# A pointwise convolution whose start is rearranged: weights, first rows and their queues

## The chip, the core and the metric

The kernel runs on one core of a Trainium2 chip. Its engines work side by side and are ordered by semaphores: TensorE (PE) multiplies matrices, VectorE (DVE) and ScalarE (ACT) move and convert data, GpSimd (POOL) does small side work, and SyncE (SP) issues most of the transfers. ScalarE can issue transfers too, on a queue of its own. The metric is the device time of one execution in microseconds (us). It is measured several times and the median is taken.

## The reference: what is computed

A depthwise convolution with a 1x1 window is a scaling of each channel, so the whole reference is one matrix product with scaled rows:

```python
# x: (1, 384, 384, 384) bf16, dw: (1, 1, 384), pw: (384, 384)
out = x * dw[0, 0]                              # k = 1: no neighbours, a scale for each channel
out = jnp.einsum('bhwc,cd->bhwd', out, pw)      # 147456 rows of 384, times a 384x384 matrix
```

There are N = 147,456 rows. The kernel folds `dw` into `pw` once and then multiplies every row of `x` by the folded 384x384 matrix.

## The kernel before

The rows are worked on in supertiles of 512 rows; there are NS = 288 of them. For each one the DVE transposes `x` (32x32 blocks of 32-bit words, so two bf16 channels stay together), TensorE runs 48 matmuls that accumulate in four PSUM banks, and ScalarE copies the result to SBUF as bf16. Both the transposed tile `T` and the PSUM tile `PS` exist twice. Groups of supertiles are loaded as chunks of `x` and stored from tiles `O`:

```python
def _groups(n_super):
    head, tail = [[1, 1, 2, 2, 4]], [[6, 4], [4, 1, 1, 1, 1]]
    mid = n_super - sum(map(sum, head + tail))
    return head + [[LMAX]] * (mid // LMAX) + tail      # LMAX = 10; a number is supertiles in a chunk
```

Before the first supertile the weights have to be made. `pw` comes in thirds of 128 rows, `dw` as one row. TensorE turns the `dw` row into a column, one matmul for each third; the DVE multiplies a selection matrix by it (`sel_w`); TensorE multiplies `sel_w` by `pw`, which scales, picks and replicates the rows. That gives six pieces (third k, parity r), which are copied from PSUM to `w_r`.

```python
# SyncE's queue, and one transfer on ScalarE's
nc.scalar.dma_start(dw_row[:], ...).then_inc(s_dw, 16)
nc.sync.dma_start(pw_n[:, 0], pw[0:P, :]).then_inc(s_pw, 16)
nc.sync.dma_start(pw_n[:, 1:3], pw[P:C, :]...).then_inc(s_pw2, 16)
load_x(0)
...
# TensorE, in order of its program
idle_work(4)                       # 16 matmuls on constants
nc.tensor.wait_ge(s_dw, 16)
... three matmuls of dw_row -> PS[1][:, 0, D:D+3], then_inc(s_df)
idle_work(2)
nc.tensor.wait_ge(s_pw, 16)
times = {(2, 0): 2, (2, 1): 2}     # the last third's matmuls are run twice
for k in range(3):
    if k == 1: nc.tensor.wait_ge(s_pw2, 16)
    nc.tensor.wait_ge(s_sw, k + 1)             # sel_w of this third
    for r in range(2):
        if k == 2: nc.tensor.wait_ge(*w_done[r])   # PSUM is free again
        for v in [0, 1] * times.get((k, r), 1):
            nc.tensor.matmul(PS[(k + 1) % 2][:, 2 * r + v, :D],
                             lhsT=sel_w[64 * v : 64 * v + 64, k, r, :, :]..., rhs=pw_n[64 * v : 64 * v + 64, k, :], ...)
        mm.then_inc(s_w)
with nc.tensor.Fori(0, NS // 2 - 1, 1) as it: ...     # supertiles, 48 matmuls each
```

In a supertile the matmuls go through twelve steps (channel block b, parity), four matmuls in each. The waits stand in it like this:

```python
w_first = {(0, 0): [(0, 1), (1, 3)], (4, 0): [(1, 4)], (4, 1): [(1, 5)]}   # step: (engine, pieces done)
for b, par in steps:        # (0,0), (0,1), (1,0), ... (3,1), (4,0), (5,0), (4,1), (5,1)
    for q in range(4):
        if q == 0 and par == 0 and b in (0, 3): nc.tensor.wait_ge(s_t[s][b // 3], rv)   # T's halves
        if q == 0 and s == 0:
            for e, v in w_first.get((b, par), []): nc.tensor.wait_ge(s_wr[e], v)
        nc.tensor.matmul(PS[s][:, q, :D], lhsT=Ts[s][...], rhs=w_r[...], ...)
```

The pieces are copied by ScalarE, except for the second, which the DVE takes (`w_eng = [1, 0, 1, 1, 1, 1]`). The DVE's program at the start is: `sel`, the copy of `dw` out of PSUM, three `sel_w`, its piece, and then the transposes, two halves of three channel blocks for each supertile:

```python
nc.vector.tensor_copy(dw_f[:], PS[1][:, 0, D : D + 3])
for k in range(3):
    nc.vector.tensor_scalar_mul(sel_w[:, k], sel..., dw_f[:, k : k + 1]).then_inc(s_sw)
for i in range(6): w_out(i)
transposes(*order[0]); transposes(*order[1])
```

Of the kernel before, what the change touches and what calls it, by code (L numbers as in the profile page):

```python
# [8 lines left out]
F32 = mybir.dt.float32  # L9
# [3 lines left out]
LMAX = 10  # L13
# [3 lines left out]

def _groups(n_super: int):

    head, tail = [[1, 1, 2, 2, 4]], [[6, 4], [4, 1, 1, 1, 1]]  # L20
    mid = n_super - sum(map(sum, head + tail))
    assert mid > 0 and mid % LMAX == 0
    return head + [[LMAX]] * (mid // LMAX) + tail
# [3 lines left out]
def kernel(  # L27
# [12 lines left out]
    nc = tc.nc  # L40
    P = nc.NUM_PARTITIONS
    B, H, W, C = x.shape
    assert dw.shape[0] == 1 and dw.shape[1] == 1, "only k=1 depthwise supported"
    D = pw.shape[1]
# [10 lines left out]
    chunks, first = [], 0  # L55
# [13 lines left out]
    consts = ctx.enter_context(tc.tile_pool(name="consts", bufs=1))  # L69
# [4 lines left out]
    pw_n = raw[:, 0 : 3 * D].rearrange("p (k d) -> p k d", d=D)  # L74
    sel_w = raw[:, 3 * D :].rearrange("p (k r q w) -> p k r q w", r=2, q=4, w=32)
    w_k = raw[:, 0 : 2 * D].rearrange("p (r d) -> p r d", d=D)
    eye = consts.tile([P, P], BF16, name="eye")
    sel = consts.tile([P, 2, 32], F32, name="sel")
    w_r = consts.tile([P, NB, 2, D], BF16, name="w_r")
    dw_row = consts.tile([1, C], BF16, name="dw_row")  # L80
    dw_f = consts.tile([P, 3], F32, name="dw_f")
    warm = consts.tile([P, 2], F32, name="warm")

    ones = nc.const_aps.tensor(1.0, [P, D], BF16)
# [6 lines left out]
    PS = [psum.tile([P, 4, 512], F32, name=f"ps{s}") for s in range(2)]  # L91
# [5 lines left out]
    s_t = [[nc.alloc_semaphore(f"s_t{i}{h}") for h in range(2)] for i in range(2)]  # L97
# [2 lines left out]
    s_d = nc.alloc_semaphore("s_d")  # L100
    s_o = [nc.alloc_semaphore(f"s_o{i}") for i in range(NR)]
    s_dw = nc.alloc_semaphore("s_dw")
    s_pw = nc.alloc_semaphore("s_pw")
    s_pw2 = nc.alloc_semaphore("s_pw2")
    s_df = nc.alloc_semaphore("s_df")
    s_sw = nc.alloc_semaphore("s_sw")
    s_dwf = nc.alloc_semaphore("s_dwf")
    s_sel = nc.alloc_semaphore("s_sel")
    s_w = nc.alloc_semaphore("s_w")
    s_wr = [nc.alloc_semaphore(f"s_wr{e}") for e in range(2)]  # L110

    with tc.tile_critical(sync_engine=mybir.EngineType.Pool, no_gpsimd_drain=True):  # L112
# [59 lines left out]
            eng.dma_start(dst, src).then_inc(s_o[g % NR], 16)  # L172

        w_eng = [1, 0, 1, 1, 1, 1]
        w_all = [(s_wr[e], w_eng.count(e)) for e in range(2)]

        nc.scalar.dma_start(dw_row[:], dw.rearrange("a e c -> a (e c)")).then_inc(s_dw, 16)
        nc.sync.dma_start(pw_n[:, 0], pw[0:P, :]).then_inc(s_pw, 16)  # L178
        nc.sync.dma_start(pw_n[:, 1:3], pw[P:C, :].rearrange("(k p) d -> p k d", p=P)).then_inc(s_pw2, 16)  # L179
        load_x(0)  # L180

        todo = []
# [3 lines left out]
            for k in range(n_parts[t] - (first + 1 == NS)):  # L186
                todo.append((first + L * (k + 1) // n_parts[t] + 1, store, (t, k)))
        for _, f, a in sorted(todo, key=lambda a: a[0]):
            if f is load_x and chunks[a[0]][4] == LMAX and chunks[a[0]][0] == 1:
                nc.sync.wait_ge(x_of(1)[1], 16)  # L190
            if f is store and a == (0, 0):

                for _ in range(28):
                    nc.sync.wait_ge(s_pw, 16)
            f(*a)
# [7 lines left out]

        w_done = [(s_wr[e], w_eng[: i + 1].count(e)) for i, e in enumerate(w_eng)]

        w_first = {(0, 0): [(0, 1), (1, 3)], (4, 0): [(1, 4)], (4, 1): [(1, 5)]}

        def w_ps(i):
            return PS[0 if i in (2, 3) else 1][:, 2 * (i % 2) : 2 * (i % 2) + 2, :D]
# [4 lines left out]
        def supertile(s, rv):  # L214
            for b, par in steps:
                for q in range(4):
                    if q == 0 and par == 0 and b in (0, 3):
                        nc.tensor.wait_ge(s_t[s][b // 3], rv)
                    if q == 0 and s == 0:
                        for e, v in w_first.get((b, par), []):  # L220
                            nc.tensor.wait_ge(s_wr[e], v)
                    mm = nc.tensor.matmul(  # L222
                        PS[s][:, q, :D],
                        lhsT=Ts[s][32 * q : 32 * q + 32, b, par::2],
                        rhs=w_r[32 * q : 32 * q + 32, b, par, :],
                        start=(b, par) == steps[0],
                        stop=(b, par) == steps[-1],
                        tile_position=(32 * q, 0),
                    )
                    if (b, par) == steps[0] and q == 0:  # L230
                        mm._wait_ge(s_a[s], rv)
                    if (b, par) in ((2, 1), (5, 1)) and q == 3:
                        mm.then_inc(s_pe)


        def idle_work(n):
            for _ in range(n):
                for i in range(4):
                    nc.tensor.matmul(  # L239
                        PS[0][:, 2 * (i % 2) + i // 2, :D],  # L240
                        lhsT=ones[32 * i : 32 * i + 32, 0:P],
                        rhs=ones[32 * i : 32 * i + 32, :],
                        start=True,
                        stop=True,
                        tile_position=(32 * i, 0),
                    )

        idle_work(4)

        nc.tensor.wait_ge(s_dw, 16)  # L250
        for k in range(3):
            mm = nc.tensor.matmul(
                PS[1][:, 0, D + k : D + k + 1],
                lhsT=dw_row[:, P * k : P * k + P],
                rhs=ones[0:1, 0:1],
                start=True,
                stop=True,
            )
# [2 lines left out]
        nc.tensor.wait_ge(s_pw, 16)  # L261
        times = {(2, 0): 2, (2, 1): 2}
        for k in range(3):
            if k == 1:
                nc.tensor.wait_ge(s_pw2, 16)
            nc.tensor.wait_ge(s_sw, k + 1)
            for r in range(2):
                if k == 2:
                    nc.tensor.wait_ge(*w_done[r])

                for v in [0, 1] * times.get((k, r), 1):
                    mm = nc.tensor.matmul(  # L272
                        PS[(k + 1) % 2][:, 2 * r + v, :D],
                        lhsT=sel_w[64 * v : 64 * v + 64, k, r, :, :].rearrange("p q w -> p (q w)"),
                        rhs=pw_n[64 * v : 64 * v + 64, k, :],
                        start=True,
                        stop=True,
                        tile_position=(64 * v, 0),
                    )
                mm.then_inc(s_w)  # L280
# [22 lines left out]
        for m in range(4):  # L303
# [14 lines left out]
            out=eye[:],  # L318
            in_=ones[:, 0:P],
# [12 lines left out]
        for n in range(4):  # L332
            for g in range(4):
                x_b = Xl[quads[g], n, 256:384].rearrange("p (b c) -> p b c", c=64)
                nc.gpsimd.tensor_copy(Xk[quads[n], g:8:4, :], x_b).then_inc(s_xk)  # L335
                nc.gpsimd.tensor_copy(Xk[quads[n], 8 + g : 24 : 4, :], Xl[quads[g], :, 64 * n : 64 * n + 64]).then_inc(s_xk)  # L336
        for s in range(2):
            nc.scalar.copy(warm[:, s : s + 1], nc.const_aps.tensor(0.0, [P, 1], F32)).then_inc(s_a[s])  # L338

        def transposes(t, j):  # L340
            g, i, off, first, L = chunks[t]
            jj = first + j
            s = jj % 2
            if jj + 1 == NS:
                nc.vector.wait_ge(s_xk, 32)
                Tw = Ts[s][:].bitcast(U32).rearrange("p b (m w) -> p (b m) w", w=32)
                for v in range(2):
                    blocks = slice(12 * v, 12 * v + 12)
                    ins = nc.vector.transpose(out=Tw[:, blocks], in_=Xk[:, blocks].bitcast(U32))  # L349
                    ins._wait_ge(s_pe, 2 * (jj - 2) + v + 1)  # L350
                    ins.then_inc(s_t[s][v])
                return
            X, sem, n = x_of(t)
            Xw = X.bitcast(U32).rearrange("p (k l) c -> p k l c", l=L)
            Tw = Ts[s][:].bitcast(U32).rearrange(
                "p b (k i) -> p b k i" if t < 2 else "p b (i k) -> p b k i", k=4
            )
            for h in range(2):
                if h == 0 and j == 0:
                    nc.vector.wait_ge(sem, n)  # L360
                ins = nc.vector.transpose(  # L361
                    out=Tw[:, 3 * h : 3 * h + 3],
                    in_=Xw[:, :, j, 96 * h : 96 * h + 96].rearrange("p k (b w) -> p b k w", w=32),
                )
                if jj >= 2:
                    ins._wait_ge(s_pe, 2 * (jj - 2) + h + 1)
                ins.then_inc(s_t[s][h])
# [6 lines left out]
        def w_out(i):  # L374
            e, k, r = w_eng[i], i // 2, i % 2
            out, in_ = w_r[:, 2 * k : 2 * k + 2, r, :], w_ps(i)
            o = nc.vector.tensor_copy(out, in_) if e == 0 else nc.scalar.copy(out, in_)  # L377
            o._wait_ge(s_w, i + 1)
            o.then_inc(s_wr[e])
# [3 lines left out]
            out=sel[:],  # L383
            in_=eye[:].rearrange("p (v w r) -> p r w v", v=2, r=2),
            op=mybir.AluOpType.add,
            axis=mybir.AxisListType.X,
        ).then_inc(s_dwf)
        nc.vector.wait_ge(s_df, 1)
        nc.vector.tensor_copy(dw_f[:], PS[1][:, 0, D : D + 3]).then_inc(s_dwf)
        nc.vector.wait_ge(s_dwf, 2)  # L390
        for k in range(3):
            nc.vector.tensor_scalar_mul(
                sel_w[:, k], sel[:].unsqueeze(2).to_broadcast([P, 2, 4, 32]), dw_f[:, k : k + 1]
            ).then_inc(s_sw)
        for i in range(6):
            w_out(i)
# [65 lines left out]
```

## Time and profile before

| what | value |
|---|---|
| median of three runs | 573.81 us (573.74 to 574.17) |
| span of the profiled execution | 571.9 us |
| TensorE busy | 567.0 us (99%) |
| VectorE busy | 505.4 us (88%) |
| ScalarE busy | 418.4 us (73%) |
| DMA, mean over the span | 397 GB/s |
| first matmul of the main loop starts | 6.52 us |
| matmuls of the main loop (line L222) | 13,776, 559.8 us busy |

A line such as L222 is a line of the kernel's source. In the timeline a row gives the start, the stretch it covers, the engine, the line, the operation with what it writes and reads, how many instructions were merged, and in brackets how long the engine was idle before and which event ended that. PEld is the loading of weights into TensorE's array; engine names with a q are queues that issue transfers.

### The profile page before, as it was taken

To read this page: it belongs to the slowest core of one execution; us is meant where nothing else is said; L and a number is where in the kernel's file an instruction comes from. 1 tells how busy PE (TensorE), PEld (TensorE's weight loads), DVE (VectorE), ACT (ScalarE), POOL (GpSimd) and SP (SyncE) were. 2 spreads that over 40 slices of the span, in tenths; PEclk is the share of its full clock that TensorE was granted. 3 is DMA by queue.
4 is the path that set the end of the run, shared out by engine and by line. 5 is a ranking of instruction groups with operands and counts; after the bars stand their busy time and mean duration, and the time that the engine had idled before them with its cause. 6 is when DMAs were issued, how large, how long until landed. Compare 5 with 4: busy or idle time off the path is not lost.

```text
span 571.9 us, 29705 instructions
## 1 busy us (share of the span) xinstructions
PE 567.0 (99%) x13843; PEld 380.0 (66%) x13843; DVE 505.4 (88%) x586; ACT 418.4 (73%) x298; POOL 13.9 (2%) x41
## 2 busy tenths in 40 slices
PE   9999999999999999999999999999999999999997
PEld 4666666666666666666666666666666666666664
DVE  6889889889889889889889889889889889889885
ACT  6777777777777777777777777777777777777775
POOL 2042000000000000000000000000000000000000
PEclk9999999999999999999999999999999999999999
DMA  8999999999999999999999999999999999998677
GB/s 328 445 393 414 426 416 428 437 426 411 430 416 420 388 396 432 388 390 396 433 382 396 418 415 408 397 416 414 395 403 428 387 394 402 420 393 351 285 287 263
DMA packets 26740, 226.88 MB, mean 397 GB/s; under 512 B 1385, under 2 KB 7274, under 8 KB 22890
## 3 DMA queue, kind: packets, MB, share of 16 engines
q1 hardware_dynamic: 25796, 225.91, 97.4%
q10 hardware_dynamic: 934, 0.89, 0.4%
q14 instruction: 9, 0.07, 0.0%
q8 instruction: 1, 0.02, 0.0%
HBM read 113.54 MB, written 113.25 MB: 397 GB/s over the span
## 4 chain that ended last, share of the span: by engine, by line
PE 98%; DMA 1%; SPq 0%; DVE 0%; issue 0%; ACT 0%; POOLq 0%
PE ps L222 98%; DMA X<-in_x_dram 1%; PE ps L307 0%; PE ps L295 0%; DVE T L361 0%; ACT O L416 0%; SPq L179 0%; SPq L178 0%; SPq L457 0%; POOLq L112 0%; POOLq L446 0%
## 5 line engine op out<-in xcount | busy, mean ns | idle before, releaser
L222 PE MATMUL ps<-w_r,T 32*128 32x384 bf16 x13776 | 559.8, 321 | 0.2 <-DVE T L361 0.2
L361 DVE STREAM_TRANSPOSE T<-X 128x384 uint32<-128x384 uint32 x572 | 498.1, 874 | 58.2 <-DMA X<-in_x_dram 2.1
L421 ACT CAST O<-ps 128x1536 bf16<-128x1536 f32 x286 | 411.4, 1438 | 147.0 <-PE ps L222 147.0
L222 PEld LDWEIGHTS ps<-w_r,T 32*128 32x128 bf16 x13776 | 377.2, 93 | 183.1 <-issue 0.9
L336 POOL COPY Xk<-Xl 32x256 bf16<-32x256 bf16 x16 | 6.3, 394 | 0.0
L335 POOL COPY Xk<-Xl 32x128 bf16<-32x128 bf16 x16 | 4.6, 287 | 25.2 <-DMA Xl<-in_x_dram 24.3
L377 ACT CAST w_r<-ps 128x768 bf16<-128x768 f32 x5 | 3.6, 820 | 0.8 <-PE ps L272 0.8
L330 POOL COPY raw<-w_r 32x768 bf16<-32x768 bf16 x4 | 3.3, 819 | 6.4 <-ACT w_r L377 6.2
L239 PE MATMUL ps<-const-bfloat16-1.0 32*128 32x384 bf16 x24 | 2.2, 516 | 1.1 <-PEq L446 1.1
L272 PE MATMUL ps<-raw 64*128 64x384 bf16 x16 | 2.9, 513 | 0.1
L338 ACT ACT_TABLE_LOAD x1 | 1.3, 1283 | 1.5 <-PEq L446 1.5
L272 PEld LDWEIGHTS ps<-raw 64*128 64x128 bf16 x16 | 0.8, 113 | 2.2 <-DMA raw<-in_pw_dram 1.2
L412 DVE CAST O<-ps 128x384 bf16<-128x384 f32 x2 | 1.0, 552 | 1.4 <-PE ps L222 1.4
L361 DVE STREAM_TRANSPOSE T<-Xl 128x384 uint32<-128x384 uint32 x2 | 1.8, 876 | 0.2
L239 PEld LDWEIGHTS ps<-const-bfloat16-1.0 32*128 32x128 bf16 x24 | 0.7, 117 | 1.4 <-issue 1.4
L349 DVE STREAM_TRANSPOSE T<-Xk 128x384 uint32<-128x384 uint32 x2 | 1.2, 578 | 0.5 <-PE ps L222 0.4
L382 DVE TENSOR_REDUCE sel<-eye 128x64 f32<-128x128 bf16 x1 | 0.3, 290 | 1.5 <-POOL eye L317 1.5
L307 PE MATMUL ps<-raw,T 128*128 128x384 bf16 x8 | 1.5, 327 | 0.0
L416 ACT CAST O<-ps 128x384 bf16<-128x384 f32 x2 | 1.0, 478 | 0.7 <-PE ps L307 0.7
L377 DVE CAST w_r<-ps 128x768 bf16<-128x768 f32 x1 | 1.0, 958 | 0.5 <-PE ps L272 0.5
L416 DVE CAST O<-ps 128x384 bf16<-128x384 f32 x2 | 1.1, 558 | 0.1
L411 ACT CAST O<-ps 128x384 bf16<-128x384 f32 x2 | 0.9, 482 | 0.5 <-PE ps L222 0.5
(13 smaller groups left out, 4.5 us busy)
## 6 DMA issues: line engine op xcount, KB each, us to landing
X<-in_x_dram SPq DMA_DIRECT2D x26, 3840.0 KB, 21.9
out_dram<-O SPq DMA_DIRECT2D x26, 3840.0 KB, 27.9
X<-in_x_dram SPq DMA_DIRECT2D x3, 1536.0 KB, 18.5
out_dram<-O SPq DMA_DIRECT2D x4, 768.0 KB, 7.7
out_dram<-O SPq DMA_DIRECT2D x2, 1536.0 KB, 13.7
X<-in_x_dram SPq DMA_DIRECT2D x1, 2304.0 KB, 20.2
out_dram<-O SPq DMA_DIRECT2D x1, 2304.0 KB, 11.1
X<-in_x_dram SPq DMA_DIRECT2D x4, 384.0 KB, 4.4
```

The source lines that it names most:

```text
L222: mm = nc.tensor.matmul(PS[s][:, q, :D], lhsT=Ts[s][32 * q : 32 * q + 32, b, par::2], rhs=w_r[32 * q : 32 * q + 32, b, par, :], start=(b, ...
L239: nc.tensor.matmul(PS[0][:, 2 * (i % 2) + i // 2, :D], lhsT=ones[32 * i : 32 * i + 32, 0:P], rhs=ones[32 * i : 32 * i + 32, :], start=True ...
L272: mm = nc.tensor.matmul(PS[(k + 1) % 2][:, 2 * r + v, :D], lhsT=sel_w[64 * v : 64 * v + 64, k, r, :, :].rearrange("p q w -> p (q w)"), rhs ...
L307: mm = nc.tensor.matmul(PS[1][:, m, :D], lhsT=Tk[:, P * (m + 2) : P * (m + 3), par], rhs=w_k[:, par, :], start=False, stop=par == 1,)
L330: nc.gpsimd.tensor_copy(w_k[quads[n]], w_r[quads[n], n]).then_inc(s_wk)
L335: nc.gpsimd.tensor_copy(Xk[quads[n], g:8:4, :], x_b).then_inc(s_xk)
L336: nc.gpsimd.tensor_copy(Xk[quads[n], 8 + g : 24 : 4, :], Xl[quads[g], :, 64 * n : 64 * n + 64]).then_inc(s_xk)
L338: nc.scalar.copy(warm[:, s : s + 1], nc.const_aps.tensor(0.0, [P, 1], F32)).then_inc(s_a[s])
L361: ins = nc.vector.transpose(out=Tw[:, 3 * h : 3 * h + 3], in_=Xw[:, :, j, 96 * h : 96 * h + 96].rearrange("p k (b w) -> p b k w", w=32),)
L377: o = nc.vector.tensor_copy(out, in_) if e == 0 else nc.scalar.copy(out, in_)
L416: o = (nc.scalar.copy if n % 2 else nc.vector.tensor_copy)(Ov[:, n, j, :], PS[s][:, n, :D])
L421: a = nc.scalar.copy(Ov[:, :, j, :], PS[s][:, :, :D])
```

## The change

The change touches the preparation and the sizes of the first chunks. The loop over supertiles has the same matmuls.

- The last third of `pw` leaves SyncE's queue. ScalarE issues it, after it has seen the first third land. The first rows of `x` thereby stand behind two thirds of `pw` on SyncE's queue, and not behind three.
- The first half of the first supertile's transposes is cut into three, one for each channel block, so that the first matmuls can start after one block.
- `dw` is read by the three `sel_w` multiplications out of PSUM, without the copy to SBUF. It lies in another bank, which the third of `pw` in the middle writes later, so TensorE waits for all of `sel_w` ahead of that piece.
- The fourth piece of `w_r` is copied by the DVE and ScalarE, one half each.
- One round of four matmuls on constants is taken out.
- Chunks at the head: 1, 1, 1, 1, 2, 4 and then 5, 5 supertiles, in place of 1, 1, 2, 2, 4 and then 10.

```diff
-    head, tail = [[1, 1, 2, 2, 4]], [[6, 4], [4, 1, 1, 1, 1]]
+    head, tail = [[1, 1, 1, 1, 2, 4], [5, 5]], [[6, 4], [4, 1, 1, 1, 1]]
...
-        nc.sync.dma_start(pw_n[:, 1:3], pw[P:C, :].rearrange("(k p) d -> p k d", p=P)).then_inc(s_pw2, 16)
+        nc.sync.dma_start(pw_n[:, 1], pw[P : 2 * P, :]).then_inc(s_pw2, 16)
...
-        w_first = {(0, 0): [(0, 1), (1, 3)], (4, 0): [(1, 4)], (4, 1): [(1, 5)]}
+        w_first = {(0, 0): [(0, 2), (1, 3)], (4, 0): [(1, 4)], (4, 1): [(1, 5)]}
...
+                        if par == 0 and b in (1, 2):
+                            nc.tensor.wait_ge(s_tb, b)
...
-        idle_work(4)
+        idle_work(3)
...
-                PS[1][:, 0, D + k : D + k + 1],
+                PS[0][:, 3, D + k : D + k + 1],
...
-            if k == 1:
-                nc.tensor.wait_ge(s_pw2, 16)
+            if k >= 1:
+                nc.tensor.wait_ge(s_pw2 if k == 1 else s_pw3, 16)
             nc.tensor.wait_ge(s_sw, k + 1)
             for r in range(2):
+                if (k, r) == (1, 1):
+                    nc.tensor.wait_ge(s_sw, 3)
...
             nc.scalar.copy(warm[:, s : s + 1], ...)
+        nc.scalar.wait_ge(s_pw, 16)
+        nc.scalar.dma_start(pw_n[:, 2], pw[2 * P : C, :]).then_inc(s_pw3, 16)
...
+                if h == 0 and jj == 0:
+                    for b in range(3):
+                        x_b = Xw[:, :, 0, 32 * b : 32 * b + 32]
+                        nc.vector.transpose(out=Tw[:, b], in_=x_b).then_inc(s_tb if b else s_t[0][0])
+                    continue
...
+            if i == 3:
+                o = nc.vector.tensor_copy(out[:, 1], in_[:, 1])
+                o._wait_ge(s_w, i + 1)
+                o.then_inc(s_wr[0])
+                out, in_ = out[:, 0], in_[:, 0]
...
-        nc.vector.tensor_copy(dw_f[:], PS[1][:, 0, D : D + 3]).then_inc(s_dwf)
-        nc.vector.wait_ge(s_dwf, 2)
...
-                sel_w[:, k], sel[:].unsqueeze(2).to_broadcast([P, 2, 4, 32]), dw_f[:, k : k + 1]
+                sel_w[:, k], sel[:].unsqueeze(2).to_broadcast([P, 2, 4, 32]), PS[0][:, 3, D + k : D + k + 1]
```

More of the change, by code (lines that the diff above doesn't have):

```diff
@@ L80 @@
     dw_row = consts.tile([1, C], BF16, name="dw_row")
-    dw_f = consts.tile([P, 3], F32, name="dw_f")
     warm = consts.tile([P, 2], F32, name="warm")
@@ L102 @@
     s_dw = nc.alloc_semaphore("s_dw")
+    s_tb = nc.alloc_semaphore("s_tb")
     s_pw = nc.alloc_semaphore("s_pw")
     s_pw2 = nc.alloc_semaphore("s_pw2")
+    s_pw3 = nc.alloc_semaphore("s_pw3")
     s_df = nc.alloc_semaphore("s_df")
@@ L174 @@
         w_eng = [1, 0, 1, 1, 1, 1]
-        w_all = [(s_wr[e], w_eng.count(e)) for e in range(2)]
+        w_all = [(s_wr[0], 2), (s_wr[1], 5)]
         nc.scalar.dma_start(dw_row[:], dw.rearrange("a e c -> a (e c)")).then_inc(s_dw, 16)
         nc.sync.dma_start(pw_n[:, 0], pw[0:P, :]).then_inc(s_pw, 16)
-        nc.sync.dma_start(pw_n[:, 1:3], pw[P:C, :].rearrange("(k p) d -> p k d", p=P)).then_inc(s_pw2, 16)
+        nc.sync.dma_start(pw_n[:, 1], pw[P : 2 * P, :]).then_inc(s_pw2, 16)
         load_x(0)
@@ L188 @@
         for _, f, a in sorted(todo, key=lambda a: a[0]):
-            if f is load_x and chunks[a[0]][4] == LMAX and chunks[a[0]][0] == 1:
+            if f is load_x and chunks[a[0]][:2] == (1, 0):
                 nc.sync.wait_ge(x_of(1)[1], 16)
@@ L239, in idle_work @@
                     nc.tensor.matmul(
-                        PS[0][:, 2 * (i % 2) + i // 2, :D],
+                        PS[1][:, 2 * (i % 2) + i // 2, :D],
                         lhsT=ones[32 * i : 32 * i + 32, 0:P],
@@ L387 @@
         ).then_inc(s_dwf)
+        nc.vector.wait_ge(s_dwf, 1)
         nc.vector.wait_ge(s_df, 1)
-        nc.vector.tensor_copy(dw_f[:], PS[1][:, 0, D : D + 3]).then_inc(s_dwf)
-        nc.vector.wait_ge(s_dwf, 2)
         for k in range(3):
             nc.vector.tensor_scalar_mul(
-                sel_w[:, k], sel[:].unsqueeze(2).to_broadcast([P, 2, 4, 32]), dw_f[:, k : k + 1]
+                sel_w[:, k], sel[:].unsqueeze(2).to_broadcast([P, 2, 4, 32]), PS[0][:, 3, D + k : D + k + 1]
             ).then_inc(s_sw)
```

## The prediction, made before the changed kernel was run

> **What bounds the kernel now.** I read the page's chain that ended last first, because one engine is busy 99% of the span and I want to know whether that is work or waiting.
>
> ```profile
> PE 98%; DMA 1%; SPq 0%; DVE 0%; issue 0%; ACT 0%; POOLq 0%
> L222 PE MATMUL ps<-w_r,T 32*128 32x384 bf16 x13776 | 559.8, 321 | 0.2 <-DVE T L361 0.2
> ```
>
> The second line is the group of main matmuls. 559.8 / 13,776 is 40.6 ns for one, or 1.95 us for the 48 of a supertile, and in front of all of them TensorE idled 0.2 us. So once the loop has begun it never waits, and the span is (start of the loop) + 559.8 + (a tail of some 5.6 us). The change leaves the loop's matmuls and the tail as they are. Only the start of the loop, at 6.52 us, is open to it. Next I asked for the chain in order of time, window 0 to 10 us:
>
> ```profile
> 0.96 0.39 SPq L178
> 1.35 0.06 issue
> 1.41 0.41 SPq L179
> 1.82 0.05 issue
> 1.87 3.94 DMA X<-in_x_dram
> 5.81 0.02 issue
> 5.84 0.59 DVE T L361
> 6.43 0.09 issue
> 6.52 3.59 PE ps L222 x70
> ```
>
> The columns are start, duration, what. The chain goes through two issues of pw, the transfer of the first rows (issued 1.87, landed 5.81), and one transpose of three blocks. The third view is the timeline of the first 9 us, for how close the others are behind this chain:
>
> ```profile
> 2.67 0.16 DVE L389 COPY dw_f<-ps 128x3 f32<-128x3 f32 x1 [0.91 <-PE ps L252]
> 2.83 0.28 ACT L338 COPY warm<-const-float32-0.0 128x1 f32<-128x1 f32 x2
> 2.87 0.88 DVE L392 TENSOR_SCALAR raw<-sel,dw_f 128x256 bf16<-128x256 f32 x3
> 3.34 0.16 PEld L272 LDWEIGHTS ps<-raw 64*128 64x128 bf16 x4 [0.74 <-DMA raw<-in_pw_dram]
> 3.91 3.61 ACT L377 CAST w_r<-ps 128x768 bf16<-128x768 f32 x5 [0.80 <-PE ps L272]
> 4.23 0.96 DVE L377 CAST w_r<-ps 128x768 bf16<-128x768 f32 x1 [0.48 <-PE ps L272]
> 5.24 0.38 PEld L272 LDWEIGHTS ps<-raw 64*128 64x128 bf16 x4 [0.26 <-DVE w_r L377]
> ```
>
> Two other chains end just before 6.52. ScalarE copies its five pieces back to back at a pitch of 0.70 us (asked for singly they start at 3.91, 4.61, 5.29, 5.99, 6.67), and the third of them, without which the loop may not start, ends at 6.11. TensorE's last weight matmul starts at 5.8 and, at 0.52 us, ends at 6.32. So whatever makes the rows earlier gains 0.2 to 0.4 us at most before something else holds the loop, unless those move as well. The change does move them; the question is whether all three.
>
> [...]the 384 KB of Xl, issued on ScalarE's queue at 24.32 us while SyncE's was full, were in use only at 35.41, 11.1 us later, against 3.94 for the same size at the start. [...]the first third of pw took 2.0 us from issue to landing and the other two together 2.5. [...]the 16 weight matmuls take 474 to 524 ns up to 6.3 us, the first main ones 350 at 6.52, then 321 at full rate; the granted clock of the page shows 1.0 throughout and doesn't show this switch.
>
> **The change part by part.**
>
> *dw from PSUM, one round of idle work less.* Removed: the copy of 0.16 us and the 0.04 us behind it. sel_w then starts about 2.65 in place of 2.87, its first is ready at 3.0 in place of 3.22, and TensorE's first weight matmul goes at about 3.12 in place of 3.37 (the first third of pw is there at 0.96 + 2.0 = 2.96). I assume that a scalar read from PSUM costs nothing more. So the pieces move 0.22 us forward: ScalarE's first starts at 3.7, its second at 4.4, and both can be served, as the second third of pw, with 96 KB less behind it, should land around 3.5 in place of 3.91.
>
> *Fourth piece by two engines.* In place of one copy of 0.82 at 5.29: after its second copy (ready to go on at 3.7 + 2 x 0.70 = 5.1) ScalarE copies 384 columns, about 0.48 us (the 128x384 copies of the tail take 478 to 482 ns). The DVE, done with its piece at 4.0 + 0.96 = 4.97, takes 0.55 for its half (tail: 552 to 558). Both end near 5.55, against 6.11: 0.55 us earlier.
>
> *First rows behind two thirds of pw.* 192 KB in place of 288 KB go ahead of them. Two thirds took 0.94 us longer to land than one (3.91 - 2.97), so one third less is worth 0.3 to 0.45 us; the second issue and the rows' own keep their places within 0.03. From that comes off what ScalarE's third takes when it breaks in among the rows, up to 0.15. I put the landing at 5.5 in place of 5.81.
>
> *Three transposes.* A half of 384 words takes 579 ns, and the second half follows after 0.54. As three of 128 words I estimate 0.3 for the first: the part that does not shrink is taken as 0.18 us (the 3-word copy took 0.157), and the rest is a third of 0.4. The first block is ready at 5.5 + 0.03 + 0.31, plus the 0.09 seen before the matmul: the loop could begin at about 5.93. The later blocks come every 0.27, and TensorE needs one every 8 x 0.0406 = 0.325, so they follow in time; the second half is at worst 0.1 late.
>
> Up to here the change is worth 6.52 - 5.93 = 0.6 us.
>
> *The last third of pw on ScalarE's queue.* ScalarE sees the first third land at 2.96 and issues at once. The earliest landing, with nothing in its way, is 2.98 + 2.0 = 5.0. But the rows stand before it on every DMA engine and go on beside it, with packets of 3 KB against its 768 bytes. I allow 0.8 us for that (a choice: the two thirds had 0.5 more than one, Xl very much more): landing at 5.8. TensorE waits for it before the main loop, because its program has this third's matmuls first, all eight of them, as each is run twice. They run in pairs; from 4.9 to 5.8 four pairs start, 0.3 to 0.32 us apart, so all eight need 1.28 us at the slow clock and 0.65 at the fast. The loop can begin at 5.8 + 0.05 + 1.28 = 7.13 if the clock is still low, and at 6.5 if it has risen before. In the kernel before it rose somewhere between 6.1 and 6.5; kept there, two pairs run slow and two fast, and the loop begins at 6.8 to 6.85. The two last pieces then reach ScalarE from about 6.4 and 7.0 and are ready by 7.9, before the 32 matmuls (1.3 us) to their step are over, so they add nothing.
>
> *Smaller chunks.* The one long wait of the DVE for rows, 1.47 us at 24.71 for the first chunk of ten, goes away, but TensorE did not feel it: half a T was ready at 25.6, and its supertile began at 6.52 + 10 x 1.95 = 26.0. Worth nothing. The two new waits in each even supertile should cost nothing: its four waits for weights today don't make it longer than an odd one (copies at 8.72, 10.67, 12.62, 14.57, all 1.95 apart).
>
> Sum: the loop begins at 6.8 in place of 6.52, 0.3 us later; with a small share for the rivals below I write **574.0 us** against 573.81.
>
> **The rivals.** First: the last third is not late. If it lands by 5.2, or the clock is up by 5.7, the rows set the start as meant and the kernel gains 0.3 to 0.6 us: 573.2 to 573.5. For it: the third is small, 8 packets for each of 16 engines, and the second half of its matmuls is there only to keep TensorE busy, so somebody counted on it. Against it: ScalarE cannot issue before 2.96. Second: the clock rises later. In the new program TensorE has nothing to do from about 4.6 to 5.8, and [...]main matmuls run at half rate for one to three microseconds: 575 to 576. For it: the first kernel's weight matmuls were never faster than 474 ns, so its clock rose only just in time[...]. Third: ScalarE's transfer delays the rows so far that nothing is won there, which only matters if the first rival holds: 573.7 to 573.9.
>
> **Range and chances.** I give the late third 0.55, the first rival 0.3, the clock 0.15. The lower end takes in the gain, 573.2; the upper one most of a late clock, 575.1. Two per cent are 11.5 us; all that can change is inside the first 7 us, so the chances of either side are only for what I have not thought of.
>
> **What the next profile would show.** If I am right, the weight-load rows of line L272's successor have an idle stretch of about 1 us released by DMA from pw, ending near 5.8, and the chain in order of time runs through ScalarE's transfer and not through X. The rows should land near 5.5 and the first small transpose take about 0.3. The pieces' third and fourth copy should be over near 5.6. After its first supertile the loop should keep 1.95 us. Wrong would be: the chain still going through X and the transpose (first rival), matmuls of 500 ns in the main loop (second), or a difference that is not in the first 10 us at all.

## The result and the profile after

The changed kernel takes **578.94 us** (six runs, 578.42 to 579.72) against 573.89 us for the kernel before on the same chip (573.74 to 574.17). The ratio is 1.0088, with a 95% interval of 1.0075 to 1.0101: slower by 5.05 us, and far outside the range that was given. The profiled spans are 576.8 and 571.9 us.

First the page's groups of the changed kernel, for the main matmuls and for the weight matmuls. The columns are busy time, mean of one in ns, then idle time before them and what ended it.

```profile
L225 PE MATMUL ps<-w_r,T 32*128 32x384 bf16 x13776 | 561.4, 322 | 0.0
L277 PE MATMUL ps<-raw 64*128 64x384 bf16 x16 | 3.1, 512 | 3.7 <-DMA raw<-in_pw_dram 3.7
```

The loop itself has grown by some 1.5 us (559.8 before), although it has the same 13,776 matmuls, and in front of the weight matmuls TensorE now idles 3.7 us for a transfer of `pw`. The chain that ended last, in order of time (start, duration, what), shows how the start is now bound:

```profile
2.83 0.17 ACT warm L343
3.00 5.40 DMA raw<-in_pw_dram
8.40 0.05 issue
8.45 1.46 PE ps L277 x8
9.91 561.36 PE ps L225 x12985
571.27 0.65 PE ps L300 x16
```

The loop's line in the same view of the kernel before:

```profile
6.52 559.85 PE ps L222 x12053
```

The rows of `x` are gone from the chain. In their place stands the last third of `pw`, issued by ScalarE at 3.00 and landed 5.40 us later. Then come the eight matmuls of that third, and only then the loop: at 9.91 in place of 6.52. That is 3.39 us of start and 561.36 - 559.85 = 1.51 us of loop, 4.90 together, which is the whole difference of the two spans.

The timeline of the changed kernel, for the parts that went as meant:

```profile
2.65 0.89 DVE L408 TENSOR_SCALAR raw<-sel,ps 128x256 bf16<-128x256 f32 x3 [0.88 <-PE ps L255]
4.70 1.18 ACT L394 CAST w_r<-ps 128x768 bf16<-128x768 f32 x2 [0.21 <-PE ps L277]
5.02 0.56 DVE L390 CAST w_r<-ps 128x384 bf16<-128x384 f32 x1
5.75 0.70 DVE L371 STREAM_TRANSPOSE T<-X 128x128 uint32<-128x128 uint32 x3 [0.17 <-DMA X<-in_x_dram]
```

By 6.1 us everything that the loop's first matmuls read is there; only the last third's own matmuls, ahead of them in TensorE's program, are missing. Why that third took so long is seen in the DMA view of two stretches, 3.0 to 6.3 us and 6.3 to 8.4 us (queue, packets, MB, share of the 16 engines; q1 is SyncE's queue, q10 ScalarE's):

```profile
q1 hardware_dynamic: 363, 0.99, 91.8%
...
q1 hardware_dynamic: 234, 0.70, 90.5%
q10 hardware_dynamic: 144, 0.10, 14.3%
```

In the first stretch q10 moved nothing at all (it has no row), though the transfer was issued at 3.00. All of its 128 data packets and 16 semaphore writes lie in the second. Up to 6.3 us it did not share the engines with the rows; it stood behind them.

And the loop's extra 1.5 us, in the durations (min/median/max in ns) of main matmuls in two stretches, from 9.9 us and from 14 us:

```profile
L225 PE MATMUL ps<-w_r,T x16: 495/522/523, 9.8 to 10.8; 32*128 32x384 bf16 x16
...
L225 PE MATMUL ps<-w_r,T x32: 320/321/322, 13.7 to 14.9; 32*128 32x384 bf16 x32
```

Low clock and full clock stand here for these two paces: 522 ns for one, with groups of four 0.32 us apart, against 321 ns and 0.16 us. The granted clock of the profile is 1.00 in both stretches and doesn't show the difference. The loop started at the low clock and reached the full one only at about 13.0. The clock had not been up before the wait either, as the weight matmuls ahead of it show:

```profile
L277 PE MATMUL ps<-raw x8: 477/510/525, 3.1 to 4.5; 64*128 64x384 bf16 x8
```

So the hole of 3.47 us in TensorE's work (4.98 to 8.45) did not take a full clock away; the question is whether it put off its rise.

### The profile page after: what moved, and what is told of

The parts are those of the page before. It is cut to its first block, busy times and chain, and to the rows that moved or that the text cites. A ratio compares the mean times of both kernels' runs of the same rounds, so it can differ in the third digit from the quotient of the medians.

```text
span 576.8 us, 29707 instructions
## 1 busy us (share of the span) xinstructions
PE 568.5 (99%) x13839; PEld 337.3 (58%) x13839; DVE 508.4 (88%) x588; ACT 418.6 (73%) x298; POOL 13.9 (2%) x41
## 4 chain that ended last, share of the span: by engine, by line
PE 98%; DMA 1%; ACT 0%; ACTq 0%; issue 0%; POOLq 0%
PE ps L225 97%; DMA raw<-in_pw_dram 1%; PE ps L277 0%; PE ps L312 0%; ACT L343 0%; PE ps L300 0%; ACTq L178 0%; ACT O L432 0%; ACT warm L343 0%; ACTq L473 0%; POOLq L113 0%; POOLq L462 0%
## 5 line engine op out<-in xcount | busy, mean ns | idle before, releaser
L225 PE MATMUL ps<-w_r,T 32*128 32x384 bf16 x13776 | 561.4, 322 | 0.0
L225 PEld LDWEIGHTS ps<-w_r,T 32*128 32x128 bf16 x13776 | 335.0, 93 | 226.7 <-issue 2.3
L394 ACT CAST w_r<-ps 128x768 bf16<-128x768 f32 (+1 forms) x5 | 3.5, 737 | 4.2 <-PE ps L277 4.2
```

Of the source, the lines that this page charges most:

```text
L225: mm = nc.tensor.matmul(PS[s][:, q, :D], lhsT=Ts[s][32 * q : 32 * q + 32, b, par::2], rhs=w_r[32 * q : 32 * q + 32, b, par, :], start=(b, ...
```

## The experiments

The theory from here on (A): all of the loss is the last third's transfer. It has two halves: why it is late (A1, it stands behind what SyncE has put on the same DMA engines, against A2, ScalarE's queue is slow in itself), and why the loop is slow (C, the hole that the wait made kept the clock low, against D, some input is missing). The rival B puts a part of the loss on the other changes. Each run is compared with the kernel before on its own chip (medians of 573.99 to 574.16 us); the ratio given is not that of the two medians and can differ from it by some 0.001.

**The last third back on SyncE's queue, the rest of the change kept.**

```diff
-nc.sync.dma_start(pw_n[:, 1], pw[P : 2 * P, :]).then_inc(s_pw2, 16)
+nc.sync.dma_start(pw_n[:, 1:3], pw[P:C, :].rearrange("(k p) d -> p k d", p=P)).then_inc(s_pw2, 16)
...
-nc.scalar.wait_ge(s_pw, 16)
-nc.scalar.dma_start(pw_n[:, 2], pw[2 * P : C, :]).then_inc(s_pw3, 16)
```

> The changed kernel with one part undone: the last two thirds of pw come in one transfer on SyncE's queue, ahead of the first rows, as before; the other parts of the change stay. Theory A (all of the 5.05 us is the last third: it lands at 8.40, and TensorE, idle from 5.0 to 8.4, runs the first main matmuls at the low clock): the third lands near 3.9, the rows near 5.8, the first block is transposed by 6.15 and the loop begins near 6.25, so 573.6 us, 0.2 to 0.3 under the kernel before. Theory B (another part carries some of the loss, for example the two waits in each even supertile or the many small chunks): 575 or more.

Measured: 573.85 us, ratio 1.0001 (0.9993 to 1.0009). Its chain:

```profile
3.16 2.91 PE ps L276 x16
6.07 559.77 PE ps L224 x13776
```

The whole loss is gone, so B falls. The loop begins 0.45 us earlier than in the kernel before, as the other parts were meant to do, and its profiled span is 571.4 against 571.9. The median, however, is no better: the execution profiled was the fastest of fourteen, which spread from 573.29 to 575.16.

**The last third alone moved, everything else as before.**

```diff
-nc.sync.dma_start(pw_n[:, 1:3], ...).then_inc(s_pw2, 16)
+nc.sync.dma_start(pw_n[:, 1], pw[P : 2 * P, :]).then_inc(s_pw2, 16)
+nc.scalar.wait_ge(s_pw, 16)
+nc.scalar.dma_start(pw_n[:, 2], pw[2 * P : C, :]).then_inc(s_pw3, 16)      # TensorE waits for s_pw3 at k == 2
```

> The kernel before with one part of the change alone: the last third of pw on ScalarE's queue after the first third has landed. Theory A: the third lands 3 us or more after the rows, about 8.4, the loop begins near 9.9 at the low clock, 578.5 to 579.5 us. Theory B: at most half of the loss, 574.5 to 576.5 us.

Measured: 580.16 us, ratio 1.0109 (1.0091 to 1.0127).

```profile
2.93 6.08 DMA raw<-in_pw_dram
...
10.52 560.71 PE ps L223 x13776
```

The third landed after 6.08 us, at 9.01, and the loop began at 10.52. One part of the change brings all of the loss. That it brings somewhat more than the whole change did (1.0088) is not shown, as the intervals overlap.

**The last third on ScalarE's queue, but at once.**

```diff
 nc.scalar.dma_start(dw_row[:], ...).then_inc(s_dw, 16)
+nc.scalar.dma_start(pw_n[:, 2], pw[2 * P : C, :]).then_inc(s_pw3, 16)
...
-nc.scalar.wait_ge(s_pw, 16)
-nc.scalar.dma_start(pw_n[:, 2], pw[2 * P : C, :]).then_inc(s_pw3, 16)
```

> The changed kernel, with the last third still on ScalarE's queue but issued right behind dw, at about 1.5 us, without the wait for the first third. Theory A1 (the third is late because the rows' descriptors are already on the same DMA engines when it comes, and are served first): at 1.5 us they are not, it lands by about 4.2, and the rows by 5.8; the loop begins near 6.2, 573.4 to 573.7 us. Theory A2 (a transfer on ScalarE's queue is slow beside a busy SyncE queue whenever it is issued): it lands past 6.5 and the time is 576 to 578 us.

Measured: 573.84 us, ratio 1.0000 (0.9992 to 1.0008). The same transfer on the same queue lands within 2.3 us when it is issued at 1.53 (in the last run below, which issues it at the same moment, within 3.4) and needs 5.4 when it is issued at 3.00. So it is not the queue (A2 falls); what was issued before it is left. The loop began at 6.08, yet its first matmuls ran slow, although TensorE had no hole ahead of it:

```profile
L226 PE MATMUL ps<-w_r,T x16: 494/522/523, 6.0 to 7.0; 32*128 32x384 bf16 x16
```

**SyncE holds the second chunk back until the first has landed.**

```diff
+if f is load_x and a[0] == 1:
+    nc.sync.wait_ge(x_of(0)[1], 16)
```

> The changed kernel, with SyncE holding back the second chunk of rows until the first has landed; the last third is issued as in the changed kernel, at 3.0 us. Theory A1 (the third has to wait for what was put on SyncE's queue before and shortly after it, 8 packets on each engine for each chunk): only the first chunk stands before it, so it lands at 5.3 to 6.0 in place of 8.40, and the loop begins at 6.7 to 7.3; the second chunk is later by 2.5 us, which may show as a wait at the second supertile; 574.3 to 576 us. Theory A2 (ScalarE's queue is slow by itself): still past 7.5, 578 us or more.

Measured: 575.63 us, ratio 1.0034 (1.0024 to 1.0044).

```profile
2.96 2.74 DMA raw<-in_pw_dram
5.70 0.05 issue
5.74 1.46 PE ps L279 x8
7.20 561.52 PE ps L227 x12716
```

With one chunk of 384 KB before it in place of several, the third needs 2.74 us in place of 5.40. A1 stands: some 2.7 us, the difference of these two profiles, are the wait behind further rows. The hole in TensorE's work is now 1.17 us long (4.57 to 5.74), and the loop still ran at the low clock until 10.6; its busy time, 561.52, is as long as after the hole of 3.47 us.

**The change with the old chunk sizes.**

```diff
-head, tail = [[1, 1, 1, 1, 2, 4], [5, 5]], [[6, 4], [4, 1, 1, 1, 1]]
+head, tail = [[1, 1, 2, 2, 4]], [[6, 4], [4, 1, 1, 1, 1]]
...      # and SyncE's wait ahead of the first chunk of ten, as in the kernel before
```

> The changed kernel with the chunk sizes of the kernel before (1, 1, 2, 2, 4 and 10). Theory A1 (the third on ScalarE's queue is served after the chunks that SyncE has already put before the engines, so their size counts): the third chunk of rows is 768 KB in place of 384, the third lands at 8.9 to 9.4, and the time is 0.5 to 1.2 us above the changed kernel's on the same chip, 579.4 to 580.4 us. Rival: the wait does not depend on what the chunks hold, landing and time as the changed kernel's within 0.4 us.

Measured: 579.97 us, ratio 1.0096 (1.0081 to 1.0111). The changed kernel itself, run beside it:

> The changed kernel itself, unaltered, as the measure for the next two on the same chip: the last third issued at 3.0 lands at 8.3 to 9.1, the main matmuls take 561 us or more, 578.4 to 579.7 us.

It took 579.12 us, ratio 1.0086 (1.0071 to 1.0100). The third's line in the chain, with the old chunks:

```profile
3.03 8.04 DMA raw<-in_pw_dram
```

and in the chain of the changed kernel beside it:

```profile
2.95 5.18 DMA raw<-in_pw_dram
```

The third waits 8.04 us, more than was expected, when the third chunk of rows holds 768 KB, and 5.18 when it holds 384. The execution profiled was the longest of its four, 582.24, so 8 us is the upper end, and the intervals of the two ratios overlap. The direction is that of A1: the kernel before with the third alone moved, which has the old chunks too, waited 6.08, and both lie above the four profiles of the changed kernel's chunks (4.47 to 5.86 us, with the two runs that fill the hole below). That the size of a chunk counts is thus likely; by time it is not shown.

**The last third by SyncE, between the first and the second chunk.**

```diff
 load_x(0)
+nc.sync.dma_start(pw_n[:, 2], pw[2 * P : C, :]).then_inc(s_pw3, 16)
...
-nc.scalar.wait_ge(s_pw, 16)
-nc.scalar.dma_start(pw_n[:, 2], pw[2 * P : C, :]).then_inc(s_pw3, 16)
```

> The changed kernel, but the last third is issued by SyncE, on the same queue as the rows, between the first and the second chunk. Theory A1 (on ScalarE's queue the third was served only after nearly all that SyncE had put before the engines, two chunks): here it has one chunk before it, lands about 0.3 to 0.5 us after the first rows, at 5.9 to 6.3, and the loop begins at 7.2 to 7.6, at the low clock because of the hole in TensorE's work: 575.0 to 576.3 us. Theory E (being behind the rows is cheap when the queue is right): the loop begins by 6.6 at the full clock and the time is 573.5 to 574.2 us.

Measured: 575.98 us, ratio 1.0019 (1.0003 to 1.0035).

```profile
2.34 3.33 DMA raw<-in_pw_dram
5.67 0.05 issue
5.72 1.46 PE ps L278 x8
7.18 561.42 PE ps L226 x12050
```

The third landed at 5.67, right behind the rows and even earlier than I had put it, and the loop began at 7.18. So the place behind the rows costs something on either queue, because TensorE's program has this third's matmuls ahead of the loop. Of the eight runs three took 573.91 to 574.30 and five 575.77 to 576.74. The profiled one, with a loop of 561.42 us, is one of the five. Whether the three found the clock up in time is not shown, as none of them was profiled.

**TensorE kept busy in the hole.**

```diff
 if k == 2:
+    nc.tensor.wait_ge(*w_done[0])
+    for _ in range(14): ...     # two matmuls on constants, 64 rows each, into PSUM banks that are free
```

> The changed kernel, and while TensorE waits for the last third it runs 14 pairs of matmuls on constants into two free PSUM banks (from about 4.5 us on; 0.32 us a pair at the low clock, 0.16 at the full one). The third still lands near 8.4. Theory C (the hole in TensorE's work costs as much again as it is long lost: the clock has to be earned anew, 1.5 us in the loop and 0.65 us in the last third's eight matmuls): those eight take 0.65, the loop begins near 9.1 and runs at full rate from its start, so its busy time is 559.8 in place of 561.4 and the time 576.3 to 577.0 us. Theory D (the slow first matmuls have another cause than the hole, such as weights or rows not ready): the time stays at 578.5 to 579.5 us.

> The changed kernel with 14 pairs of matmuls on constants in TensorE's hole, a second time and beside the changed kernel on the same chip, as in the first run the third landed 0.5 us later than in the profile of the changed kernel and the last store took 1.5 us longer than in any other, which hid the size. Theory C: loop 559.8 us, the third's eight matmuls 0.65 to 0.85, together 2.0 to 2.3 us less than the changed kernel for the same landing; medians of the two apart by 1.3 to 2.3 us. Theory D: apart by less than 0.7.

First time: 578.23 us, ratio 1.0065 (1.0046 to 1.0083), above the time that was expected. Second time, beside the changed kernel: 576.94 us, ratio 1.0056 (1.0042 to 1.0071), 2.2 us less than the 579.12 there. The chain of the second:

```profile
3.06 4.47 DMA raw<-in_pw_dram
7.52 0.05 issue
7.57 0.82 PE ps L292 x8
8.39 559.76 PE ps L225 x13776
```

and the matmuls on constants of that execution:

```profile
L254 PE MATMUL ps<-const-bfloat16-1.0 x28: 322/325/335, 4.5 to 6.7; 64*128 64x384 bf16 x28
```

The eight matmuls take 0.82 in place of 1.46 us and the loop 559.76 in place of 561.4 to 561.8. D falls: the inputs are as before, only the clock differs. It was up from the first matmul of the filling, and it stayed up over the 0.56 us of idleness behind the filling (0.88 in the first run). In the first run both terms came out the same (0.82 and 559.76), but the third landed at 8.89 and the last store took 1.5 us longer than elsewhere, which hid most of it. The third's landing scatters by more than a microsecond from run to run (7.52, 8.12, 8.40 and 8.89 in the four profiles of this arrangement), so the sizes in the profile are surer than the difference of the medians. In the profile of this second run the third also landed 0.6 us earlier than beside it.

**The short hole filled.**

```diff
+if f is load_x and a[0] == 1: nc.sync.wait_ge(x_of(0)[1], 16)
 if k == 2:
+    nc.tensor.wait_ge(*w_done[0]); ...     # 4 pairs of matmuls on constants
```

> The run that holds back the second chunk, with 4 pairs of matmuls on constants in the hole of 1.2 us (4.5 to 5.7) that TensorE has there. Theory C[...]: the clock is up by 6 to 7.3 us, the loop begins at 6.6 to 7.0, and 575.63 becomes 574.1 to 574.9 us. Theory D ([...]the slow matmuls there have another cause, such as the late second chunk): 575.3 us or more.

Measured: 575.32 us, ratio 1.0030 (1.0012 to 1.0049). By time this cannot be told from the 1.0034 without the filling. In the profile the loop runs at the full clock from its first matmul, at 7.71:

```profile
7.71 559.76 PE ps L227 x13776
```

So the loop is 1.76 us shorter than with the hole. Half a microsecond of it was paid back: in this execution the second third landed only at 4.39, the filling began at 5.25 and ended after the last third was there, and the loop began 0.5 us later. The profiled spans still differ by 1.1 us (573.2 against 574.3), while the medians lie 0.3 apart, on two chips; the execution profiled with the hole was 0.64 us above its median. So the profile agrees with the clock's theory, but the time does not: it lies where D had put it, and the gain is not shown by it.

**Two versions meant to be faster.** The first puts the first chunk on ScalarE's queue and takes one doubling out:

```diff
+load_x(0, nc.scalar)          # behind dw, at 1.5 us
...                            # all of pw by SyncE; ScalarE issues none of it
-times = {(2, 0): 2, (2, 1): 2}
+times = {(2, 0): 2}
```

> A version meant to be faster: all of pw on SyncE's queue ahead of the other rows as in the kernel before, the first chunk of rows on ScalarE's queue at 1.5 us (0.4 us earlier, and beside pw, not behind it), one of the two doublings of the last third's matmuls taken out, the rest as in the changed kernel. Theory A: the rows land near 5.0 to 5.3, the loop begins at 5.6 to 5.8. If the clock is not yet up then, half of what is gained against the 6.0 of the run with the third on SyncE's queue is lost again: 573.2 to 573.7 us. The rival: the rows, sharing the engines with pw, push the second and third thirds of pw back, by up to 0.5 us, and the gain is eaten: 573.8 to 574.5 us.

Measured: 576.21 us, ratio 1.0031 (1.0018 to 1.0044), slower.

```profile
1.41 4.39 DMA raw<-in_pw_dram
5.80 0.05 issue
5.84 1.78 PE ps L276 x10
7.62 0.09 issue
7.71 561.52 PE ps L224 x13110
```

The rival was right and too mild: the last two thirds of `pw`, now issued beside the rows, landed at 5.80 (4.39 us after their issue; before, 2.5), and the loop began at 7.71. What the rows gained is not shown: their first transpose starts at 7.18, without a wait for them.

The second is the kernel with the last third issued at once, with one doubling less:

> A version meant to be faster: the last third on ScalarE's queue at once, at 1.5 us, and only one of the last third's two groups run twice, so that TensorE is free for the loop at about 5.7 in place of 6.0; the rest as in the changed kernel. The loop can begin at 5.8 (rows landed at 5.4, first block 0.31, 0.09). Theory C: the clock is not up at 5.8 in most executions, so half of the 0.7 us gained against the kernel before is lost again: 573.3 to 573.8 us, a ratio of 0.9990 to 0.9998, at the edge of what can be told. Rival: the start doesn't matter at all because the clock alone decides: 573.9 to 574.2 us.

Measured: 574.47 us, ratio 1.0001 (0.9988 to 1.0014), a median above both expectations.

```profile
1.87 4.00 DMA X<-in_x_dram
5.88 0.02 issue
5.90 0.32 DVE T L370
6.22 0.09 issue
6.32 561.12 PE ps L226 x12054
```

Here `dw` came late (its first matmul at 2.64, in place of 2.27 in the run with both doublings), the third needed 3.4 us from its issue, and the rows landed at 5.88, so the loop began at 6.32, and at least its first 28 matmuls took a median of 522 ns; the loop's 561.12 us ate the start. The runs spread from 573.03, the lowest of all in the study, to 575.89. No version was found that beats the kernel before.

## Why the prediction was wrong, point by point

- **What bounds the kernel** was read rightly: only the start of the loop is open, and the waits added to each even supertile cost nothing. In the changed kernel ScalarE's copies come at 13.63, 15.58, 17.53, 19.48, still 1.95 apart.
- **dw from PSUM**: right. `sel_w` starts at 2.65 as said, takes 0.350 each against 0.348, and the first weight matmul starts at 3.15 (said: 3.12).
- **Fourth piece**: right. Said near 5.55; the DVE's half ends at 5.58. ScalarE's ended at 5.88 in the first profile, as the second third of `pw` landed at 4.1, and at 5.55 in the second.
- **First rows**: said 5.5, seen 5.72 in one profile of the changed kernel; in the other the first transpose starts at 5.33 without a wait for them. Over the profiles in which two thirds go ahead of the rows and the last one behind them it lies at 5.34 or before in three and at 5.82 in the latest, and in the two with all three ahead at 5.81 and at 5.50 or before, so the 0.3 us that I took a third to be worth is not told apart from the scatter. The 0.94 us from which I took it also held the 0.45 us by which the second transfer was issued later.
- **Three transposes**: right, 0.311 and then 0.269 for each (said 0.3 and 0.27).
- **The last third**: the mechanism was named, and that it would set the start. The step that failed is its landing, "I allow 0.8 us for that (a choice ...): landing at 5.8". It landed at 8.40. I took the third's packets to move beside the rows' from the start, an estimate that no view of before showed; the trace shows none of them before 6.3, and holding back the second chunk brings the wait from 5.40 to 2.74. The sum should have put the first two chunks before it and the third beside it, and not the first alone: in the trace the second chunk's last packet begins at 5.76 and the first one of the last third of `pw` at 6.39. The row that showed this, Xl's 11.1 us behind a full queue, was in my hands, and I did not use it for the size. That is 2.6 of the 4.6 us by which the sum was short (4.9 measured in the spans, 0.3 forecast).
- **The clock**: I let the eight matmuls run half slow (1.0 us) and the loop at full rate. Measured 1.46 and a loop longer by 1.51: another 2 us. Two errors are in this. The hole was 3.47 us because the landing was mis-sized; and that a hole of 1.2 us (4.6 to 5.8, as forecast) would not hold the clock down was my estimate, which no view of before showed. Over all profiles, the last group of main matmuls at the low clock starts at 10.0 us or later in the seven with a hole of 1.1 us or more in TensorE's work, and at 8.6 us at most (in the latest of them, the last run, estimated from the end of its first supertile at 9.79) in the other seven, which have no idle stretch above 0.5 us before the clock rises. The rise itself scatters by some 4 us among the latter, so no single profile proves it; the two groups do not overlap. I had given this rival 0.15 as an alternative to the late third, but it follows from it: the later the third, the longer TensorE is idle.
- **Smaller chunks**: "worth nothing" held for the wait at 24.71, which is gone and moved nothing. That the sizes may decide how long the third waits was not seen; in the profiles with the smaller chunks it waited less.
- **The 0.6 us that the other parts were to bring**: the start did move, to 6.07 in the run with the third back on SyncE's queue, 0.45 us earlier, but the median did not follow (1.0001, 0.9993 to 1.0009). In two such profiles the first matmuls ran at half rate (a median of 522 ns), and the runs scatter over 2 us. That the start's gain goes into the clock is what those profiles show; that it accounts for the tie of the medians is argued from the scatter and not settled.

## What to carry to other kernels

A transfer issued from a second engine need not run beside the first queue from its start (here no packet of it moved for 3.4 us): count all that was issued before it, and if a small transfer gates the start, try to issue it before the bulk and not when it is needed (landed within 2.3 and 3.4 us here, against 5.40). Here a wait on TensorE in the first microseconds cost twice, 3.39 us as the later start and 1.51 us as the clock that rose later, so a rival of the kind "the clock rises later" belongs in the sum of the late case, not beside it. And look whether the work that waits stands in an engine's program ahead of work that could go: here the last third's matmuls held up a loop whose first 32 matmuls do not need them. No run moved them behind these.

## What the runs showed of the hardware that was not expected

The same 96 KB on ScalarE's queue took 2.3 and 3.4 us when it was issued ahead of the rows, 2.6 and 2.74 with one chunk of rows before it, 4.5 to 5.9 in the four profiles that issue rows and third as the changed kernel does, and 6.1 and 8.0 with the old chunks. In the changed kernel's first profile no packet of it moved for 3.4 us (issued at 3.00, the first one at 6.39), where I had expected packets beside the rows' from the start. Once begun it did move beside them: from 6.3 to 8.4 us q10 took 14.3% of the 16 engines and q1 90.5%. The full clock was first seen at 4.5 us in one profile, at 6.0 to 7.6 us in five others without a hole of 1.1 us, and at some 8.9 us (estimated as above) in one with 0.37 us of idleness on the way; TensorE's first matmul starts at 1.12 in the four profiles that show it. A hole of 1.1 us before the rise went with a loop at the low clock until 10.0 us or later; one of 0.88 us behind the rise left the clock up. What decides when it rises no run here shows.
